# Linear attention followed by a phase-mixing block on one core: two more batches' x, and one more batch's u, turned by DMA instead of TensorE, part of the absolute values on ScalarE, and a new instruction order

## The chip, the core and the metric

The kernel runs on one core of a Trainium2 chip. The metric is the device time of one execution in microseconds (us), here the median of a few executions. The core has five engines with queues of their own, each of which works strictly in order: TensorE (PE, with its weight loads as PEld), VectorE (DVE), ScalarE (ACT), GpSimd (POOL) and SyncE (SP). SP computes nothing; it issues DMA transfers. POOL computes a little and issues the transfers that change the data type. An engine that waits for another holds up everything behind it in its own queue, and the order in those queues is what most of this change alters.

## The reference

All of it is done for 8 batches with 8 heads, 576 rows and 64 columns per head; the channel width C is 512.

```python
kv  = einsum('bhsd,bhse->bhde', k, v)          # 64x64 per head
o   = einsum('bhsd,bhde->bhse', q, kv)
x   = o / sqrt(mean(o*o) + 1e-6) * g_norm      # per head; then heads side by side: 576 x 512
th  = x @ w_theta
zr, zi = x * cos(th), x * sin(th)
y   = w_tok_r @ zr + w_tok_i @ zi              # mixes the 576 rows
u   = x + y
out = u + maximum(u @ w_ch, 0)
```

## The kernel before, in words

A batch's 576 rows are cut into four tiles of 128 rows (numbered 0 to 3) and a tail of 64 rows (tile 4, kept with its two halves of columns on 128 partitions). Each batch goes through these steps; the word in brackets is the name used below, followed by the tile that the profile shows and the line.

- The transfers of k and v (tiles kt and vt, lines 200 and 206 for the full rows and the tail rows) go out on SP into two buffers each, so batch b can be loaded once the key-value product of batch b-2 is done. q comes by POOL (qh and qe, lines 212 and 218), which turns it into fp16, into three buffers.
- The key-value product (kv, line 285, 80 small matmuls per batch) and its copy out of PSUM (kbd, lines 307 and 309).
- q is turned: by TensorE in batches 0 and 1, by a DMA transpose on SP from batch 2 on (qD, line 330).
- The raw product (raw, lines 344 and 353) into one of only two PSUM buffers; its square on ACT (sqb, 366), the row sums on DVE (ss, 375), the inverse root on POOL (rt, 382), and the scaling on DVE that gives x (405 and 414) and frees the PSUM buffer.
- x is turned so that its channels lie on partitions. Batches 0 to 4 do it with four TensorE transposes per full tile and two for the tail (xps, line 302). Batches 5 to 7 do it with DMA transposes on SP (xd, line 433): one for tiles 0 and 1, one for tiles 2 and 3, one for the tail. A copy that multiplies by g follows (xT, lines 257 and 259).
- The phase product (th, lines 464 and 467); then on ACT the rounding to whole turns (pt, 480), on DVE the remainder (arg, 486) and its absolute value (arg, 494), on ACT sine (sc, 502) and cosine (sc, 509), on DVE the product with x (zm, 531). The tail's parts are moved by small POOL transfers (zt, 537).
- The token mix (y, line 554): eight output pieces per batch, each made of nine matmuls that are issued in three parts of three. The first part needs the z of tiles 0 and 1, the second that of tile 2, the third tile 3 and the tail. DVE adds x and gives u (wn, 569).
- The channel product (v, lines 464 and 467). Its sum with u needs u turned back: by four TensorE transposes (ups, line 302) and a copy on ACT (us, 588), or, for the full tiles of batches 5 and 6, by a DMA transpose on SP (ud, line 596) while ACT takes max(v, 0) out of PSUM (vs, 601). DVE adds the two (617 and 612) and SP stores the result (625 and 629).

One list of numbers, TURNS (lines 29 to 81), sets the order. Each number is a task of the list above for one batch and tile; `play` calls the tasks in that order, and so each engine's queue gets its share in that order. A letter behind a number (A, D, P) moves a task that may run on several engines to ACT, DVE or POOL; `r14` means 14 matmuls without use, which keep TensorE's clock up. A task that is called early waits in its queue until its inputs and its buffer are there, and holds up what stands behind it.

`XD` (line 144) is the first batch whose x is turned by DMA, `UD` (line 145) the batches whose u is. xd and qD take their buffers from the same ring of four.

Of the kernel before, what the change touches and what calls it, by code (L numbers as in the profile page):

```python
# [12 lines left out]
AFT = mybir.ActivationFunctionType  # L13
# [17 lines left out]
36 55 50 42 51 37 52 38A 12 56D 53 54 21 63 71 57 64D 43 72 58 73 65 74 44 r2 137 133 59 45 75 46 60  # L31
66 76 138A 134A 61 62 67 77 68 79 89 125 90D 69 70 126 80 r5 91 107 92 108 81D 78 93 98 82 116 117D
94 99 83 95 118 100 129 127 84 85 119 96 86 101 128 87 130 102 120 97 121 88 109 139 141 171 159 122
110 104 123 140 142A 103 124 111 112 105 28 29 26 22 206 27 207 208 30 201 163 135 131 202 113 136
114 106 132D 115 203 204 155 r2 172 160 161 229 173 164 165 156 215 216 162 174 230 166 167 157 147
148 143 168 169 144 158 170 222 145 185 209 210 211 212 149 151 213 186 223D 214 146 150 152 217 231
236 153 243 218 232 237 244 219 154 220 233 205 388 366 377 187 190 175 234 357 188 221 177 192 224
191 176 178 235 225 250 226 251D 238 259 358 227 239 260D 240 193 353 354 514 355 194 356 189 195
252 180 261 196 253 181 262 228 254 245 360 361 241 255 242 263 264 268 362 363 246 256 257 265 266
364 365 247 269D 258 248 359 249 270 286 277 389 271 390 287D 278 288 182 267 391 272 273 183 279  # L40
315 367 289 274 392 275 290 393 291 276 378 311 280 292 293 281 282 379 283 323 312 319 320 430 316
324 284 368 431 294 501 525 502 536 503 504 179 285 369 317 313 318 314 380 505 370 381 321 307 308
325 303 322 326 371 304 305 309 299 300 432 310 382 403 394 433 306 404D 395D 342 301 372 383 396
373 384 397 302 374 434 435 405 347 197 508 509 510 511 406 348 436 437 385 398 407 399 408 438 198
375 386 441 440 439 506 442 295 296 344 400 343 401 513 512 409 376 387 345 402 412 515 526 297 421
422D 298 413 516 410 414 337 423 332 339 349 517 411 415 338 527 416 417 350 528 418 424 419 507 518
529 653 519 425 426 340 530 656 657 658 659 451 542 520 427 428 660 521 420 661D 522 334 537 459 452
662 523 429 543 538 333 335 524 460 453 471 472 473 551 454 539 540 531 461 455 532 552 474 673 684
346 649 650 184 651 652 533 541 456 467 457 468 469 663 534 462 458 535 470 578 327 553 664 328 554
665 579D 463 674 464 560 666 654 465 580 675 555 561D 466 676 556 557 581 558 667 582 677 562 544  # L50
563 583 564 565 685 447 448 329 490 569 545 584 686 566 567 570 585 491 443 449 444 445 546 559 678
687 450 586 446 330 688 571 690 492 668 689 547 691 572 548 669 341 821 810 336 475 679 477 726 573
568 574 727D 670 493 655 589 590 587 588 801 671 797 331 798 832 799 800 494 804 476 575 680 478 681
699 805 806 807 497 728 495 700 549 809 550 808D 496 576 729 682 701 485 692 498 672 730 577 731 480
599 600 591 811 592 593 702 481 486 683 703 822 717 607 601 812 693 705 704 694 594 602 813 814 732
733 823 696 608 603 609 604 605 595 718D 610 734 815 606 824 719 596 597 708 619 735 825 738 802 720
709 706 598 721 695 707 620 615 616 710 621 611 833 826 711 834 697 612 613 623 617 622 722 835 618
836 736 803 737 837 712 698 713 614 625 628 487 816 827 482 714 624 828 817 715 488 626 829 818 483
716 950 629 723 724 838 479 956 872 943 951 952 953 643 767 819 725 847 644 955 820 954D 763 751 764
752 768 769 765 747 748 830 749 638 957 753 831 766 770 873D 754 750 958 839 959 962 848 630 755 960  # L60
484 967 855 489 627 978 944 849 963 756 757 874 850 851 964 631 840 945 946 875 852 639 841 758 961
876 965 947 739 743 740 744 741 968 745 759 842 877 966 742 856 969 853 878 746 970 864D 879 760 640
# [3 lines left out]
895 907 897 898 899 985 904 908 983 896 993D 977 986 889 890 1096 987 900 988 1097 994 891 885 1098  # L66
892 909 1107 1099 995 1108 1018 1001 632 989 996 1109 1110 786 886 913 887 914 888 1100 997 990 1019
998 991 999 1002 1010D 782 915 910 911 1101 1020 783 916 912 1111 992 352 775 1117 637 199 1003 1118
793 937 1102 1021 1022 1023 784 1011 1004 1024 1103 1005 794 499 780 642 1123 917 796 785 648 1104
1025 1012 1119 918 928 923 1026 1013 1120 1006 1014 1105 1007 787 919 1008 924 929 1000 1132D 788  # L70
# [4 lines left out]
1160 1034 1141D 1139 1150 1142 940 1161 1162 935 1151 1152 1074 1163 1143 1164 1084 1144 1085 1069  # L75
# [27 lines left out]
def kernel(  # L103
# [12 lines left out]
    nc = tc.nc  # L116
# [24 lines left out]
    NX, NXE = 7, 4  # L141
    QD = 2

    XD = 5
    UD = (5, 6)

    ZD = 2
    NKV = 2
# [340 lines left out]
        )  # L489
        arg_sb[b, j] = arg  # L490

    def even_arg(b, j):
        arg = arg_sb[b, j]
        nc.vector.tensor_scalar(  # L494
            out=arg[:, 1, :].bitcast(I32), in0=arg[:, 0, :].bitcast(I32),
            scalar1=0x7FFFFFFF, scalar2=None, op0=ALU.bitwise_and,
# [401 lines left out]
```

## Time and profile before

| | |
|---|---|
| median of 3 executions | 221.31 us (220.44 to 221.79) |
| the profiled execution | 221.22 us, of which 219.4 us span from its first to its last instruction |
| TensorE | 204.7 us busy (93%) |
| VectorE | 175.5 us busy (80%) |
| ScalarE | 132.2 us busy (60%) |
| GpSimd | 97.4 us busy (44%) |
| moved by DMA | 43.43 MB, 198 GB/s on average |

The profile names work by line and by tile, `out<-in`. A row of the chain of waits gives a start, a duration, the engine, the tile, the line and the number of instructions. A row of the table of stretches gives for each engine the busy time with the number of instructions, then the clock that TensorE was granted and the busy share of the 16 DMA engines. That share adds up transfers that overlap on an engine, so it can pass 1. A row of SP's own instructions gives the time that SP took to issue a transfer, not the time of the transfer; the list of transfers gives the median from issue to landing.

### The profile page before, as it was taken

Reading aid. Unit: us, or ns where it says so; the run is one execution under the profiler, and the core shown is the slowest. Engines: PE = TensorE matmul, PEld = TensorE weight load, DVE = VectorE, ACT = ScalarE, POOL = GpSimd, SP = SyncE. Lnnn points to the kernel's source line nnn. Section 1 sums busy time; section 2 is a strip of 40 time slices with the busy share of each in tenths; the row PEclk is TensorE's granted clock in tenths of the full one; section 3 lists DMA queues with packets and bytes.
Section 4 is the critical chain, followed back from the end, with each engine's and each line's share of the span. In section 5 each row is a group of like instructions: output and inputs, shape, how many; then the busy total and the mean of one; then the engine's idle time right before and its main releaser. Section 6 shows DMA issues by size and latency. Waiting matters only on the chain.

```text
span 219.4 us, 5548 instructions
## 1 busy us (share of the span) xinstructions
PE 204.7 (93%) x2198; PEld 138.7 (63%) x2198; DVE 175.5 (80%) x371; ACT 132.2 (60%) x268; POOL 97.4 (44%) x102
## 2 busy tenths in 40 slices
PE   7996999899799999989999999999999999999991
PEld 2574456685466667756668866867587746756850
DVE  4029559518989989898999988999997999999662
ACT  2036589306599159663788845848765888557050
POOL 8227830004933529555749067534824544204000
PEclk9998599999999999999999999999999999999999
DMA  6999999965979999979999947996990776944474
GB/s 222 270 291 239 236 229 234 281 163 96 261 109 230 283 176 259 144 81 332 292 224 251 200 131 147 244 241 174 210 138 15 204 207 163 182 110 120 113 262 154
DMA packets 70059, 43.43 MB, mean 198 GB/s; under 512 B 39570, under 2 KB 63762, under 8 KB 70034
## 3 DMA queue, kind: packets, MB, share of 16 engines
q1 hardware_dynamic: 55602, 35.73, 65.5%
q0 software_dynamic: 14432, 7.36, 24.5%
q8 instruction: 17, 0.28, 0.5%
q14 instruction: 8, 0.07, 0.1%
HBM read 33.06 MB, written 9.44 MB: 194 GB/s over the span
## 4 chain that ended last, share of the span: by engine, by line
PE 61%; DVE 13%; DMA 8%; POOL 7%; ACT 7%; issue 2%; POOLq 0%; DVEq 0%; ACTq 0%
PE y L554 26%; PE v L464 10%; PE th L464 9%; DMA wn<-in_moe_w_tok_i_dram 8%; POOL rt L382 5%; PE kv L285 5%; DVE arg L486 2%; DVE ss L375 2%; PE ups L302 2%; PE raw L344 2%; DVE x L405 2%; DVE zm L531 2%; ACT sc L502 1%; PE v L467 1%; POOL qh L212 1%
## 5 line engine op out<-in xcount | busy, mean ns | idle before, releaser
L382 POOL TENSOR_TENSOR rt<-ss,mhalf 128x8 f32<-128x8 f32 (+1 forms) x35 | 54.9, 1573 | 80.5 <-DVE ss L375 78.8
L554 PE MATMUL y<-wT,zm 128*128 128x256 f16 (+1 forms) x512 | 76.0, 286 | 1.5 <-DVE zm L531 1.0
L554 PEld LDWEIGHTS <-zm 128*128 128x128 f16 x512 | 47.7, 98 | 16.9 <-DVE zm L531 2.5
L569 DVE SCALAR_TENSOR_TENSOR wn<-y,gcol,xT 128x256 f16<-128x256 f32 (+2 forms) x72 | 32.5, 477 | 8.2 <-PE y L554 7.6
L480 ACT ACTIVATE pt<-th 128x512 f32<-128x512 f32 (+1 forms) x40 | 21.9, 553 | 21.2 <-PE th L464 13.2
L464 PE MATMUL th<-wth,xT 128*128 128x512 f16 x128 | 32.9, 384 | 0.3 <-DVE xT L259 0.2
L464 PE MATMUL v<-wch,wn 128*128 128x512 f16 x128 | 31.6, 379 | 0.0
L486 DVE SCALAR_TENSOR_TENSOR arg<-pt,th 128x512 f32<-128x512 f32 (+1 forms) x40 | 24.9, 627 | 4.4 <-ACT pt L480 4.1
L509 ACT ACTIVATE sc<-arg,quarter 128x512 f16<-128x512 f32 (+1 forms) x40 | 27.1, 677 | 1.2 <-DVE arg L494 1.1
L502 ACT ACTIVATE sc<-arg 128x512 f16<-128x512 f32 (+1 forms) x40 | 23.4, 588 | 6.9 <-DVE arg L486 6.6
L366 ACT ACTIVATE sqb<-raw 128x512 f32<-128x512 f32 x32 | 18.6, 593 | 14.5 <-PE raw L344 13.2
L405 DVE TENSOR_TENSOR x<-raw,rt 128x512 f16<-128x512 f32 x32 | 21.8, 684 | 3.0 <-POOL rt L382 2.6
L375 DVE TENSOR_REDUCE ss<-sqb 128x8 f32<-128x520 f32 x32 | 21.8, 685 | 2.5 <-ACT sqb L366 2.3
L531 DVE TENSOR_TENSOR zm<-x,sc 128x1024 f16<-128x1024 f16 x32 | 21.8, 682 | 0.5 <-ACT sc L509 0.5
L617 DVE SCALAR_TENSOR_TENSOR us<-v,us 128x512 f32<-128x512 f32 (+1 forms) x32 | 19.4, 616 | 2.0 <-PE v L467 0.8
L307 ACT CAST kbd<-kv 64x256 f16<-64x256 f32 (+1 forms) x28 | 9.4, 335 | 18.5 <-PE kv L278 11.8
L588 ACT ACTIVATE us<-ups 128x512 f32<-128x512 f16 (+1 forms) x32 | 17.0, 541 | 4.1 <-PE ups L302 2.6
L537 POOL DMA_DIRECT2D zt<-zf x24 | 13.7, 576 | 12.2 <-PE v L467 10.9
L464 PEld LDWEIGHTS <-xT 128*128 128x128 f16 x128 | 11.5, 99 | 11.7 <-issue 1.3
L464 PEld LDWEIGHTS <-wn 128*128 128x128 f16 x128 | 11.8, 98 | 11.2 <-issue 0.6
L285 PE MATMUL kv<-vt,kt 128*64 128x64 f32 x560 | 18.3, 223 | 0.0
L554 PE MATMUL y<-wT,zt 128*128 128x320 f16 (+1 forms) x64 | 18.3, 286 | 0.0
(78 smaller groups left out, 256.5 us busy)
## 6 DMA issues: line engine op xcount, KB each, us to landing
kt<-in_k_dram SPq DMA_DIRECT2D x7, 1024.0 KB, 10.4
vt<-in_v_dram SPq DMA_DIRECT2D x7, 1024.0 KB, 8.5
out_dram<-us SPq DMA_DIRECT2D x24, 256.0 KB, 3.2
qh<-in_q_dram POOLq DMA_DIRECT2D x7, 512.0 KB, 7.7
out_dram<-vs SPq DMA_DIRECT2D x8, 256.0 KB, 2.3
zm<-in_moe_w_ch_dram SPq DMA_DIRECT2D x1, 1024.0 KB, 11.0
out_dram<-us SPq DMA_DIRECT2D x16, 64.0 KB, 2.1
kt<-in_k_dram SPq DMA_DIRECT2D x7, 128.0 KB, 6.9
```

What stands on the lines that cost most here:

```text
L285: nc.tensor.matmul(t[i * D:(i + 1) * D, hp - lo, :], kt[b % NKV][:, 2 * hp + i, j, :], vt[b % NKV][:, 2 * hp + i, j, :], start=(j == 0), s ...
L375: nc.vector.reduce_sum(out=ss[:], in_=sq_sb.pop((b, j))[:], axis=AXX)
L382: nc.gpsimd.tensor_tensor(out=rt[:], in0=ss[:], in1=mhalf[:, 0:h], op=ALU.pow)
L405: nc.vector.tensor_tensor(out=x_pair[b, p][:, :, a * HC:(a + 1) * HC].rearrange("p t (h e) -> p h t e", e=D), in0=r[:].rearrange("p (h t e ...
L464: nc.tensor.matmul(t[:], lhs(kc), w[:, kc, :], start=first, stop=last)
L480: nc.scalar.activation(out=pt[:], in_=th_ps[b, j][:], func=AFT.Copy, bias=MAGIC)
L486: nc.vector.scalar_tensor_tensor(out=arg[:, 0, :], in0=pt_sb.pop((b, j))[:], scalar=MAGIC, in1=th_ps.pop((b, j))[:], op0=ALU.subtract, op1 ...
L502: nc.scalar.activation(out=sc[:, 0, :], in_=arg_sb[b, j][:, 0, :], func=AFT.Sin, bias=0.0, scale=-TURN * SHRINK,)
L509: nc.scalar.activation(out=sc_sb[b, j][:, 1, :], in_=arg_sb.pop((b, j))[:, 1, :], func=AFT.Sin, bias=quarter[:], scale=-TURN * SHRINK,)
L531: nc.vector.tensor_tensor(out=dst, in0=x.unsqueeze(1).broadcast_to((P, 2, w)), in1=sc[:], op=ALU.mult)
L554: nc.tensor.matmul(t[:, 0:hi - lo], s, wT[:, w, lo:hi], start=n == 0, stop=n == len(z) - 1)
L569: nc.vector.scalar_tensor_tensor(out=dst, in0=y_in, scalar=gcol[:, 0:1], in1=x_in, op0=ALU.mult, op1=ALU.add,)
```

## The change

The computation stays as it is. Four things change.

1. `XD` goes from 5 to 3: x of batches 3 and 4 is turned by SP's DMA transposes too. That takes 8 full tiles and 2 tails away from TensorE (36 transposes) and adds four large and two small transposes to SP.
2. `UD` gets batch 4: its four full tiles of u are turned by DMA (16 TensorE transposes fewer, four DMA transposes more), and ACT takes max(v, 0) out of PSUM in place of copying u.
3. The absolute value may run on ACT. TURNS puts 15 of the 32 full tiles and 7 of the 8 tails there.
4. TURNS is new from batch 0's raw products on. Other choices move with it: 9 pairs of kbd copies on DVE where there were 4, 6 of the 9 copies of the turned token weights on DVE where there were 3, one of the four w_ch conversions on ACT (it was on POOL), and 30 matmuls without use in place of 38, all of them ahead of batch 0's weight transposes.

```diff
-    XD = 5
-    UD = (5, 6)
+    XD = 3
+    UD = (4, 5, 6,)
...
-    def even_arg(b, j):
+    def even_arg(eng, b, j):
         arg = arg_sb[b, j]
+        if eng == "ACT":
+            nc.scalar.activation(out=arg[:, 1, :], in_=arg[:, 0, :], func=AFT.Abs)
+            return
         nc.vector.tensor_scalar(
...
-            ab = add(f"ab{w} {b} {j}", "DVE", lambda b=b, j=j: even_arg(b, j), [ar])
+            ab = add(f"ab{w} {b} {j}", "DVE", lambda e, b=b, j=j: even_arg(e, b, j), [ar],
+                     alt=("ACT", "DVE"))
...
-0 1 8 4 5 6 7 2 18 3 9 10 11 14 15 r14 31 r15 39 32 47 13 16 17 24 25 33 40 34A 48 23 19 20 35 49 41
+0 1 8 4 5 9 6 7 10 2 11 14 15 13 18 r12 31 16 3 23 19 20 17 r13 39 32 40 47 33 35 48 34A 12 49 41 24
...
```

What the new order does to single queues is seen in two places. (The lines behind 494 are three or four higher after the change.) The first is POOL behind batch 0, where it computes the inverse roots rt of batch 1; qh and qe are loads of q, wch the conversions of w_ch, the MEMSETs clear the unused rows of k and v. Before:

```order
L218 DMA qe_73<-in_q_dram 64x4x64 x2
L259 TENSOR_SCALAR wch<-zm_77 128x512
L248 MEMSET kt_64 64x8x64
L248 MEMSET vt_66 64x8x64
L382 TENSOR_TENSOR rt<-ss,mhalf 128x8 x2
L212 DMA qh_68<-in_q_dram 128x8x256
L218 DMA qe_71<-in_q_dram 64x4x64
L382 TENSOR_TENSOR rt<-ss,mhalf 128x8 x2
```

After:

```order
L218 DMA qe_73<-in_q_dram 64x4x64
L259 TENSOR_SCALAR wch<-zm_77 128x512 x2
L218 DMA qe_71<-in_q_dram 64x4x64
L259 TENSOR_SCALAR wch<-zm_77 128x512
L382 TENSOR_TENSOR rt<-ss,mhalf 128x8 x4
L212 DMA qh_68<-in_q_dram 128x8x256
```

The two q loads that stood between the second and the third root of batch 1 now stand ahead of the first and behind the fourth.

The second place is SP where it loads batch 5 (kt_65 and vt_67, the full rows 128x8x256 and the tail rows 64x8x64). Before, the transposes of batch 4's q (qh_69, qe_72) stood ahead, and nothing but a store (out_dram) between the loads:

```order
L330 DMA_TRANSPOSE qD<-qh_69 128x8x128 x2
L330 DMA_TRANSPOSE qD<-qe_72 128x2x128
L625 DMA out_dram<-us 128x512
L200 DMA kt_65<-in_k_dram 128x8x256
L206 DMA kt_65<-in_k_dram 64x8x64
L625 DMA out_dram<-us 128x512
L200 DMA vt_67<-in_v_dram 128x8x256
```

After, all of batch 3's x transposes (xd) are among them, the first of them ahead of batch 4's q, and the next load (vt_66, batch 6) stands behind batch 4's first two:

```order
L433 DMA_TRANSPOSE xd<-x 128x8x128
L206 DMA kt_65<-in_k_dram 64x8x64
L330 DMA_TRANSPOSE qD<-qh_69 128x8x128 x2
L330 DMA_TRANSPOSE qD<-qe_72 128x2x128
L206 DMA vt_67<-in_v_dram 64x8x64
L433 DMA_TRANSPOSE xd<-x 128x8x128
L433 DMA_TRANSPOSE xd<-x 128x2x128
L628 DMA out_dram<-us 128x512
L200 DMA kt_65<-in_k_dram 128x8x256
L200 DMA vt_67<-in_v_dram 128x8x256
L433 DMA_TRANSPOSE xd<-x 128x8x128
L433 DMA_TRANSPOSE xd<-x 128x2x128
```

So batch 5's k and v are asked for only when x of batch 3 is complete. The other loads stand likewise: k of batch 6 behind the transpose of batch 4's x tiles 2 and 3, k and v of batch 7 behind that of batch 5's; and ahead of batch 3's k and v now stands v of batch 4, which waits for batch 2's key-value product. On PE, batch 1's key-value product comes behind 12 of batch 0's 24 token-mix parts, where it came behind 20.

More of the change, by code (lines that the diff above doesn't have):

```diff
@@ L29 @@
 TURNS = """
-0 1 8 4 5 6 7 2 18 3 9 10 11 14 15 r14 31 r15 39 32 47 13 16 17 24 25 33 40 34A 48 23 19 20 35 49 41
[L31 to L59, printed above, removed]
@@ new lines @@
+50 36 42 51 55 43 25 52 63 56 37D 64 38 71 26 53 72 54 65 44 201 73 66 45 46 57 58 67 74 59 68 75 60
+206 69 61 70 r5 137 207 62 125 138A 126 76 89 79 80 90D 81D 98 77 133 99D 21 78 107 134A 108 116 22
+359 91 117D 30A 82 92 93 129 83 100 94 95 84 96 208 118 130 203 86 27 85 127 97 101 141 128D 28 87
+102 109 119 358 88 103A 131 142 29 104 171 132D 105 135 120 110 159 106 139 121A 136D 122 163 111
+140 160 123 112 229 172 113 124 164 114 204 155 230D 156 115 215 236 173 237 165 216 174 157 161 209
@@ new lines @@
+274 391 275 290 311 392 183 323 291A 368 282 315 276 319 283 369 284 324 316 393 292 370 285 312 293
+353 378 294 430 320 379 355 431 514 380 313 325 314 381 321 326 317 371 299 300 318 383 295 382 189
+384 307 525 296 385 308 394 322 372 386 297 395D 194 373 301 309 302 403 342 374 396 343 501 298 375
+502 310 432 397 404D 508 433 398 347 509 652 434 400 376 510 399A 387 511 401 349 348 513D 436 197
+435A 303 512D 437 304 305 350 515 438 526 198 516 412 439 337 402 405 338 440 517 413 441 339 306
@@ new lines @@
+406 505 332 527 407 421 414 333 518 340 422 344 408 415 528 409 423 651 519 410 416 334 529 424 418
+425 327 520 654 335 521 506 426A 655 530 442 417A 656 411 507 419 657 345 653 427 531 522 346 455
+532 459 420 542 523 428 471 658D 456 659 460 648 429 472 328 463 533 660 473 524 464 534 457 474 671
+461 458 537 543D 465 462 538 682 551 544 539 535 540 552 650 545 466 559 546 661 467 662 541 468 553
+469 663 576 547A 672 554 451 664 673 452 329 184 674 548 647 470 453 556 555A 675 447 330 649 443
@@ new lines @@
+577 444 454 549 445 568D 448 665 449 550 495 683 578 450 684 496 569 446 579 560D 557 676 490 570
+475 685 561 688 491 580 686 558 581A 485 562 666 477 667 687 571 582 722 492 583 563 476 677 584 795
+497 573 478 586 336 565 800 498 587 341 564A 493 801 588 566 806 802 668 585 572A 803 697D 723D 669
+574 567 794 724 805 804D 698 331 828 725 678 597 726 598 699 575 613 817 480 700 614 615 679 702 593
+616 689 680 594 599 701A 690 600 728 670 703 595 727A 609 691 596 589 681 590 729 617 692 705 618
@@ new lines @@
+898 977 906 775 1102 978 907 770 885 899 979 777 1092 902 908 903 886 351 981 989D 887 900 990 1006
+1014 904 1093 982 991 1094 640 893 888 782 983 1095 894 992 1103 881 780 1104 882 771 883 1015 984
+781 998 895 909 1105 994 1113 1016 1096 986 1106 910 993A 896 635 911 884 995 999 776 912 1017 352
+985 783 1000 918 1018 1107 987 1007 996 784 1119 914 1001 1008 1020 1002 933 1019 1114 1009 789 1021
+1097 915 919 790 1022 1115 1026 1003 1116 924 1120D 1004 1117 1128D 988 1129 920 785 1023 925 929
```

29 lines of the change are left out of this document (20 added, 9 removed), and 17 rows, old and new, of the table TURNS.

## The prediction

> **What bounds the kernel now.** I read the page's totals and its slices first, then busy time by stretches, then the chain of waits, then SP's queue and the transfers.
>
> ```profile
> PE 204.7 (93%) x2198; PEld 138.7 (63%) x2198; DVE 175.5 (80%) x371; ACT 132.2 (60%) x268; POOL 97.4 (44%) x102
> DVE  4029559518989989898999988999997999999662
> PEclk9998599999999999999999999999999999999999
> DMA  6999999965979999979999947996990776944474
> ```
>
> TensorE is busiest, DVE close behind, the DMA slices are full for the first three quarters, and the clock drops once. A busy TensorE isn't one that works without gaps, since matmuls overlap. So I price its work and compare it with the time. These rows of the chain give the prices (its last three, and the first for the key-value product), the places of three key-value products, and one wait:
>
> ```profile
> 46.34 2.51 PE kv L285 x80
> 50.58 0.36 PE raw L344 x3
> ...
> 55.73 0.93 POOL qh L212
> 56.66 0.65 POOL qe L218
> 57.31 3.50 POOL rt L382 x2
> 60.83 0.69 DVE x L405
> ...
> 115.92 0.73 PE kv L285 x20
> ...
> 137.42 2.52 PE kv L285 x80
> ...
> 178.51 4.32 PE v L464 x20
> ...
> 199.98 8.82 PE y L554 x72
> ...
> 209.67 0.45 PE ups L302 x8
> ```
>
> A transpose costs 0.45/8 = 0.056, a token-mix part (three matmuls) 8.82/72 x 3 = 0.37, a full theta or channel product (four) 4.32/20 x 4 = 0.86 (a tail taken as half of it), a batch's key-value product 2.5; a raw product, four matmuls of a transpose's shape, 0.225. The stretches below begin at batch 0's token mix (35.3) and then at the key-value products of batches 1, 2, 3, 4, 5, 6, 7, up to the last matmul; the first two rows are the slow clock and what follows it.
>
> ```profile
> 20.60:27.50 6.90, 6.24 (x31) 3.32 (x32) 4.39 (x11) 3.23 (x7) 5.95 (x7) 0.51 1.13 238
> 27.50:34.30 6.80, 6.36 (x54) 3.73 (x52) 4.45 (x9) 6.20 (x13) 1.72 (x3) 1.00 1.28 239
> 35.30:46.30 11.00, 10.29 (x90) 7.65 (x90) 7.28 (x16) 4.91 (x9) 0.00 (x0) 1.00 1.24 268
> 46.30:59.90 13.60, 11.76 (x165) 8.13 (x166) 9.43 (x18) 6.93 (x15) 7.46 (x6) 1.00 0.65 150
> 59.90:81.60 21.70, 20.34 (x248) 14.10 (x248) 19.86 (x43) 13.86 (x29) 8.66 (x8) 1.00 1.04 197
> 81.60:90.80 9.20, 9.05 (x143) 6.61 (x141) 8.21 (x17) 9.01 (x21) 7.72 (x9) 1.00 1.17 226
> 90.80:115.90 25.10, 23.62 (x274) 16.48 (x268) 23.33 (x47) 16.26 (x33) 14.45 (x13) 1.00 1.06 225
> 115.90:137.40 21.50, 21.50 (x255) 15.70 (x254) 20.02 (x43) 14.26 (x29) 12.94 (x14) 1.00 0.89 178
> 137.40:159.70 22.30, 22.30 (x245) 15.52 (x246) 21.21 (x42) 15.72 (x32) 12.59 (x12) 1.00 0.95 215
> 159.70:214.10 54.40, 54.40 (x498) 36.58 (x496) 47.82 (x103) 33.79 (x67) 15.62 (x16) 1.00 0.64 152
> ```
>
> TensorE's work by these prices, in program order, is 9.3, 11.1, 18.6, 8.9, 22.5, 21.2, 22.2 and 54.0 us, where the stretches last 11.0, 13.6, 21.7, 9.2, 25.1, 21.5, 22.3 and 54.4. So TensorE waits 7.3 us in the first three, 2.9 in the next two, and 0.8 in the 98 us from batch 5 on, where it is the bound. The early waits are those for the chain raw, square, sums, root, x: in the chain two q loads of 0.93 and 0.65 stand between POOL's roots, and the x behind them comes at 60.83. Those waits, not TensorE's work, are the largest thing that an order can win.
>
> **The change part by part.** The sum is made against the profiled execution, 221.22 us, with a span of 219.4 and 1.8 around it; the median is 221.31, the same within 0.1.
>
> *Transposes off TensorE.* 36 of x and 16 of u, 52 x 0.056 = 2.9 us, nearly all of it behind 46 us. From batch 5 on nothing else covers this work, and before that it stands in a queue that is 94% busy: -2.9 (ends 0 and -2.9). The same work by stretches becomes 6.2, 13.4, 17.9, 11.7, 20.7, 17.2, 23.3 and 54.4. The matmuls without use that go stood in waits (for loads and for ACT) and cost nothing; what they did for the clock is a rival below.
>
> *Start.*
>
> ```profile
> L307 ACT COPY wT<-wps 128x576 f16<-128x576 f16 x6 | 3.7, 641 | 1.1 <-PE wps L643 1.0
> ```
>
> In batch 0's sine stage, where ACT is busy 6.20 of 6.80 us, it loses three copies of turned weights (0.641 each) and one of x, which DVE takes in its idle time; that is some 2 us of ACT's queue ahead of batch 0's last cosine and z. I take -1.3, ends 0 and -2.
>
> *Batch 1 sooner.* Its key-value product comes behind 12 token-mix parts instead of 20, 8 x 0.37 = 2.9 us sooner, and these eight parts now lie in the second stretch, where TensorE waited 2.5 us. The q loads leave the gap between the roots (0.93 + 0.65). So the waits of the first two stretches (1.7 + 2.5) nearly close; the 3.1 of the third stay, because DVE is 92% busy there. I take -4.1; ends 0 (DVE sets the pace anyway) and -7.3 (all waits go).
>
> *Absolute values and copies.*
>
> ```profile
> L494 DVE TENSOR_SCALAR arg<-arg 128x512 int32<-128x512 int32 (+1 forms) x40 | 15.7, 396 | 0.6
> L480 ACT ACTIVATE pt<-th 128x512 f32<-128x512 f32 (+1 forms) x40 | 21.9, 553 | 21.2 <-PE th L464 13.2 <-PE th L467 7.8
> L309 DVE CAST kbd<-kv 64x256 f16<-64x256 f32 x8 | 3.4, 421 | 3.6 <-ACT kbd L307 3.4
> ```
>
> 22 absolute values leave DVE, 22 x 0.396 = -8.7; five pairs of kbd copies come, 10 x 0.421 = +4.2, and three weight copies of about 0.45. DVE gains some 3 us net. An absolute value on ACT isn't in the trace; the nearest row is ACT's own copy of the same shape, 0.553, so ACT gets 22 x 0.553 = 12.2 and gives back about 5. ACT was 66% busy from 116 to 137 and stays under 75%. From batch 5 on TensorE covers both engines; I take 0. If that cover is gone, the cosine comes 0.16 later per absolute value, at most 3.5; if DVE is what holds batches 1 to 4, up to 3 come back. u of batch 4 trades an ACT copy for an ACT maximum of the same size: 0.
>
> *New transfers and new waits.* SP issues ten transposes more.
>
> ```profile
> 67.59 0.56 SPq L200 DMA_DIRECT2D kt<-in_k_dram  x1
> 68.27 6.66 SPq L330 DMA_TRANSPOSE qD<-qh  x1
> ...
> 132.71 1.28 SPq L433 DMA_TRANSPOSE xd<-x  x1
> ```
>
> ```profile
> DMA to landing us min/median/max: 5.9/8.5/21.2
> ```
>
> ```profile
> kt<-in_k_dram SPq DMA_DIRECT2D x7, 1024.0 KB, 10.4
> vt<-in_v_dram SPq DMA_DIRECT2D x7, 1024.0 KB, 8.5
> qD<-qh SPq DMA_TRANSPOSE x12, 5.7
> xd<-x SPq DMA_TRANSPOSE x9, 3.3
> ```
>
> The first rows are SP's queue, the next the view of line 200 (loads of k and v), the last the list of transfers. Undisturbed, a transpose costs SP 1.28 us and lands 3.3 us after its issue; right behind a 1 MB load SP took 6.66. Loads need 5.9 to 10.4 us, their median 8.5. For each wait I set the new chain against the TensorE work that stands between its start and the product that needs it:
>
> - k and v of batch 3 now go behind v of batch 4, a tail and a store, all of which wait for batch 2's key-value product: issued about 5 us behind it, landed at 13.5 to 15.4, needed after 15.4 of work (21 parts 7.7, five full products 4.3, two tails 0.9, small ones 2.5) and some 2 of waits. 0 to 1.5; I take 0.5.
> - Theta of batch 3 needs xd. From the channel product that DVE's x stands behind: four DVE steps of 0.68, a store of 0.5, landing 3.3, copy 0.7, so 7.2 against 7.8 of work. 0 to 2; 0.5. Behind it on SP, q of batch 4: 8.3 to 10.8 against 9.6, 0 to 1.5; 1.0. On DVE the copy of xd for tile 3 holds up batch 4's first x: 0 to 2.5; 0.5.
> - k and v of batch 5 wait in SP for xd of batch 3's tail: from that tail's raw product 6.0 to the issue (DVE takes it behind theta of tile 0: part and theta 1.2, pt 0.55, arg 0.63, x and queue 0.9; SP's transpose 1.3, store 0.5, two loads 1.0), 14.5 to 16.4 to the landing, against 13.7 of work (13 parts 4.8, seven full products 6.0, two tails 0.9, small ones 2.0). 0.8 to 2.7, less the waits above, which delay the product as well: 0.5.
> - k of batch 6 stands behind the transpose of batch 4's tiles 2 and 3: from the raw product 11.9 to the issue (8.3 of TensorE's work up to a token-mix piece that DVE adds first, 0.5, x 0.7, transpose 1.3, a tail's load and k 1.1), 17.8 to 22.3 to the landing (5.9 to 10.4), against 17.7 (24 parts 8.8, the key-value product 2.5, five full products 4.3, two tails 0.9, small ones 1.1). 0.1 to 4.6; 1.5. Batch 7 likewise (8.3 to the issue): 16.8 to 18.7 against 18.2; 0 to 0.5; 0.5.
>
> Together +5.0, ends 0 and about 15. Stores and the moves of zt behind these transfers fill buffers that have several us to spare.
>
> Sum: -2.9 - 1.3 - 4.1 + 5.0 = -3.3, so a span of 216.1 and a time of 217.9 us, 1.5% less.
>
> **The rivals.**
>
> *SP's queue becomes the bound (slower).* The place is 85 to 150 us, where a batch's loads, q, x and stores share SP and DMA. For it: there the DMA share is already 0.9 to 1.2; one transpose behind a load took SP 6.66 us; now xd of batch 4 stands directly behind two loads of 1 MB, and batch 6's v behind it. Against it: the share falls between bursts (0.65 and 0.89 in two stretches), and the new work is about 12 us of issuing (ten transposes at 1.2) over 100 us. The price: if four of the new transposes on the path take 3 us more than 1.28 to issue, the waits are 17 instead of 5, and the time is 229 or, where they partly overlap, about 226. It decides once the waits pass 8.3 us. The Trainium skill (VectorE: DVE Perf Modes, "Rules for kernel authors" and "The three transpose paths") speaks for this side: a 128x128 transpose belongs on TensorE where PSUM will do as the destination, at 390 ns against 1309 ns by DMA. By its figures the 52 blocks would be 68 us of transfers, an estimate; here eight blocks land in 3.3 us, so the trace doesn't agree with the size, and TensorE's 0.056 is far below its figure too.
>
> *The clock stays low longer.* At 20.6 to 27.5 the clock was 0.51 while TensorE transposed and waited; five matmuls without use stood there ahead of theta, and they are gone. If the low clock lasts another 6.9 us, some 4 us of theta, weight transposes and first token mix take twice as long, of which ACT, busy 6.20 of those 6.80 us, covers a part: 0 to +4, I take +3, so 220.9. Against it: batch 0's matmuls ahead of the low stretch are denser now. By the Trainium skill (TensorE: Matmul & The Clock Gate, "Part 4: PE-mode transpose") transposes don't count as busy for the clock; this trace agrees as far as its one low stretch holds mostly transposes.
>
> *DVE holds the early batches,* so that bringing batch 1 forward wins only 1 of the 4.1: 221.0. For it: 19.86 busy of 21.7 in the third stretch. Against it: DVE idled 3.7 of 11.0 in the first and 4.2 of 13.6 in the second.
>
> *Everything is hidden:* the waits are 0.5 instead of 5: 213.4.
>
> **How the numbers follow.** My forecast has 0.46, SP's queue 0.25, the clock 0.07, DVE 0.10, everything hidden 0.12. The forecast's own range is 215 to 220.5. Under 1% is about what a measurement of this kernel can't tell from no change; faster by more than that means under 219.1, slower means over 223.5. Faster: 0.40 of the forecast and all of the hidden case, 0.52. Within 1%: 0.06 of the forecast, 0.09 of DVE, 0.05 of the clock, 0.04 of SP's queue, 0.24. Slower: the rest, 0.24. The range leaves out the strongest form of SP's queue and the outer end of the hidden case: 213.0 to 225.0.
>
> **What would show it.** Right: batch 1's key-value product starts 4 us or more ahead of 46.3 and batch 3's 5 us or more ahead of 81.6; xps and ups rows are 52 matmuls fewer; no stretch from batch 5 on has TensorE idle over 2 us; DVE's arg row of absolute values falls to 18. Wrong: TensorE's waits in front of a key-value product are put down to a kt or vt transfer, or in front of theta to xd, with more than 8.3 us together; SP's transposes take 3 us or more to issue between 85 and 150; or a second stretch of clock 0.5 behind 27.

## The result, and the profile after the change

The changed kernel takes 222.29 us (median of 20 runs, 220.34 to 225.62), the kernel before 220.94 us beside it (median of 20, 218.89 to 222.2). The ratio is 1.0057 with a 95% interval of 1.0029 to 1.0085: 0.6% slower, within what I had called no difference, and not the 1.5% less of the forecast. A ratio here is always to the kernel before on the same chip and leaves disturbed runs out, so it can differ from the quotient of two medians.

The profiled execution of the changed kernel, 220.34 us with a span of 218.5, is the fastest of its 20 runs, so the trace shows 2 us less than the median. The page's totals, and TensorE's granted clock in 40 slices:

```profile
PE 197.7 (90%) x2138; PEld 133.2 (61%) x2138; DVE 172.8 (79%) x366; ACT 139.5 (64%) x278; POOL 95.2 (44%) x101
...
PEclk9999799999999999999999999999999999999997
```

TensorE is busy 7 us less and the span is 0.9 us shorter: nearly all that was taken off TensorE came back as waits. The stretches, cut as in the prediction (batch 0's token mix, then each key-value product), with the columns span, PE, PEld, DVE, ACT, POOL, clock, DMA share, GB/s:

```profile
33.30:40.20 6.90, 6.56 (x59) 4.85 (x58) 5.51 (x13) 5.11 (x11) 1.49 (x1) 1.00 1.35 218
40.20:54.00 13.80, 13.47 (x193) 10.35 (x194) 10.58 (x21) 6.89 (x13) 5.81 (x4) 1.00 0.92 207
54.00:73.70 19.70, 19.03 (x237) 13.05 (x231) 19.02 (x41) 13.83 (x31) 9.93 (x8) 1.00 1.02 247
73.70:85.20 11.50, 11.50 (x169) 8.26 (x165) 10.84 (x22) 10.31 (x21) 7.46 (x9) 1.00 1.02 195
85.20:111.00 25.80, 22.19 (x250) 14.88 (x248) 22.19 (x45) 18.53 (x39) 13.32 (x14) 1.00 1.13 199
111.00:129.70 18.70, 17.53 (x204) 12.67 (x204) 15.35 (x31) 15.39 (x31) 10.88 (x13) 1.00 1.09 244
129.70:155.60 25.90, 23.88 (x254) 16.35 (x254) 22.55 (x47) 16.82 (x34) 12.71 (x11) 1.00 1.08 219
155.60:213.30 57.70, 55.20 (x488) 36.06 (x490) 47.66 (x103) 35.76 (x69) 17.33 (x19) 1.00 0.76 158
```

Batch 3's key-value product starts at 73.7 where it started at 81.6, so it comes 7.9 us sooner in these two executions; some 1.5 us of that is the clock and not the order (see *Start* below). The five stretches behind it last 11.5, 25.8, 18.7, 25.9 and 57.7 us, for work that the prediction had put at 11.7, 20.7, 17.2, 23.3 and 54.4. So TensorE waits 5.1, 1.5, 2.6 and 3.3 us in the last four, where it had waited 3.7 us in all behind batch 3's product (times and work as in the prediction), and of the lead 0.9 us are left at the end. The waits that TensorE got are named by the view of waits (engine, tile, line, releaser; us in total, times, longest):

```profile
PE kv L285 <- DMA vt<-in_v_dram: 3.1, 2, 1.6
PEld kv L285 <- issue: 3.0, 3, 1.8
PE th L464 <- DVE xT L259: 2.1, 2, 1.7
PE kv L285 <- DMA kt<-in_k_dram: 0.9, 1, 0.9
```

Before, no key-value product waited for a transfer. Their chain runs through SP and the DMA engines; in the chain of waits the long pieces of the late half are transfers:

```profile
88.42 5.23 DMA xd<-x
...
110.87 6.18 DMA zt<-zf
...
122.83 6.77 DMA kt<-in_k_dram
...
145.63 9.82 DMA vt<-in_v_dram
...
175.78 3.92 DMA xd<-x
```

And SP's queue shows why k and v were asked for so late. Batch 5's stand behind the two transposes of x at 96.31, batch 6's k behind the one at 120.84:

```profile
96.31 3.76 SPq L433 DMA_TRANSPOSE xd<-x  x2
...
100.75 0.42 SPq L200 DMA_DIRECT2D kt<-in_k_dram  x1
101.21 0.68 SPq L200 DMA_DIRECT2D vt<-in_v_dram  x1
...
120.84 1.23 SPq L433 DMA_TRANSPOSE xd<-x  x1
...
122.83 0.60 SPq L200 DMA_DIRECT2D kt<-in_k_dram  x1
```

### The profile page after: what moved, and what is told of

The parts are those of the page before. It is cut to its first block, busy times and chain, and to the rows that moved or that the text cites. A ratio compares the mean times of both kernels' runs of the same rounds, so it can differ in the third digit from the quotient of the medians.

```text
span 218.5 us, 5445 instructions
## 1 busy us (share of the span) xinstructions
PE 197.7 (90%) x2138; PEld 133.2 (61%) x2138; DVE 172.8 (79%) x366; ACT 139.5 (64%) x278; POOL 95.2 (44%) x101
## 3 DMA queue, kind: packets, MB, share of 16 engines
q1 hardware_dynamic: 62578, 37.43, 72.6%
## 4 chain that ended last, share of the span: by engine, by line
PE 26%; DMA 25%; DVE 24%; POOL 8%; issue 7%; ACT 7%; SPq 1%; POOLq 0%; DVEq 0%; ACTq 0%
PE y L557 11%; DMA wnt<-in_moe_w_tok_i_dram 7%; DMA xd<-x 6%; PE kv L285 5%; DMA vt<-in_v_dram 4%; POOL rt L382 4%; PE th L464 4%; DVE x L405 4%; DMA kt<-in_k_dram 3%; DVE wn L572 3%; DVE arg L486 3%; DVE zm L534 3%; DMA zt<-zf 3%; PE v L464 3%; DVE ss L375 2%
## 5 line engine op out<-in xcount | busy, mean ns | idle before, releaser
L366 ACT ACTIVATE sqb<-raw 128x512 f32<-128x512 f32 x32 | 18.8, 594 | 10.5 <-PE raw L344 10.4
L591 ACT ACTIVATE us<-ups 128x512 f32<-128x512 f16 (+1 forms) x28 | 14.9, 536 | 14.0 <-PE ups L302 11.8
L540 POOL DMA_DIRECT2D zt<-zf x24 | 13.1, 551 | 21.7 <-PE th L464 6.4
L285 PEld LDWEIGHTS kv<-vt,kt 128*64 128x64 f32 x560 | 17.4, 138 | 4.8 <-issue 3.0
L557 PE MATMUL y<-wT,zt 128*128 128x256 f16 (+1 forms) x64 | 18.3, 286 | 0.4 <-DMA zt<-zf 0.2
L307 ACT CAST kbd<-kv 64x256 f16<-64x256 f32 (+1 forms) x18 | 6.2, 342 | 18.1 <-PE kv L278 10.6
```

Of the source, the lines that this page charges most:

```text
L285: nc.tensor.matmul(t[i * D:(i + 1) * D, hp - lo, :], kt[b % NKV][:, 2 * hp + i, j, :], vt[b % NKV][:, 2 * hp + i, j, :], start=(j == 0), s ...
L557: nc.tensor.matmul(t[:, 0:hi - lo], s, wT[:, w, lo:hi], start=n == 0, stop=n == len(z) - 1)
```

## The experiments

The kernels are numbered in the order in which they ran.

**Is the early gain real, and where is it given back?** Theory W: the gain up to batch 3 is real, and new late waits take it. Rival D: from batch 3 on other resources set the pace, so an early lead melts under any order. e1 follows the changed order up to batch 3's last key-value piece (task 511) and takes every later task in the old order, without the new transfers:

```diff
-    XD = 3
-    UD = (4, 5, 6,)
+    XD = 5
+    UD = (5, 6)
...
-376 510 399A 387 511 401 349 348 513D 436 197 435A
+376 510 399A 387 511 505 303 304 305 306 435 405
```

> The changed order up to batch 3's last kv, and from there the old order with x turned by transfers from batch 5 on and u in batches 5 and 6. Theory W (the early gain is real, and is given back by new waits from batch 4 on, for k and v and for x turned by transfers): the changed kernel starts batch 3's kv 7.9 us sooner with 1.5 us less of TensorE's work done by then, so about 6.4 us should come through: 214.5 us, 213 to 218. Rival D (from batch 3 on the DMA engines, ScalarE or VectorE set the pace whatever the order, so that an early lead always melts): 220 to 222 us.

Measured: 217.99 us, ratio 0.9891 (0.9848 to 0.9933). By the ratio 2.4 us come through, of the 6.4 that W expected (214.5 us). One reason is a seam: both copies of batch 3's kv stand behind sines and cosines on ScalarE there.

```profile
PE raw L344 <- ACT kbd L307: 2.2, 4, 1.7
```

e8 moves those two copies (tasks 513 and 512) up:

```diff
-505 303
+505 513 512 303
...
-401 513 512 409
+401 409
```

> The first experiment's kernel with the two copies of batch 3's kv moved up on ScalarE, ahead of four pieces of sines and cosines of batch 2, where its raw products waited 1.8 us. If the wait is only that seam of the two orders: 216.5 us, 215.5 to 217.5. If x or the q transposes of batch 3 end as late: 218 us.

Measured: 215.35 us, ratio 0.9759 (0.972 to 0.9797). This beats both kernels, the one before by 5.3 us, and shows that the seam alone cost 2.9. Its late stretches (columns as above):

```profile
85.10:110.10 25.00, 23.55 (x274) 16.44 (x268) 23.30 (x47) 16.20 (x33) 14.61 (x13) 1.00 1.12 221
110.10:131.60 21.50, 21.50 (x254) 15.71 (x252) 20.02 (x43) 14.25 (x29) 13.01 (x14) 1.00 0.87 192
131.60:154.00 22.40, 22.40 (x247) 15.59 (x248) 21.30 (x42) 15.82 (x32) 12.65 (x12) 1.00 0.96 214
154.00:208.30 54.30, 54.30 (x496) 36.47 (x492) 47.68 (x103) 33.61 (x67) 15.53 (x16) 1.00 0.66 152
```

From 110 on TensorE has no gap, as in the kernel before. D falls: under the old late order the lead stays.

e2 is the reverse, the old order up to batch 2's last key-value piece (task 363), then the changed one with its transfers:

```diff
-    XD = 5
-    UD = (5, 6)
+    XD = 3
+    UD = (4, 5, 6,)
...
-264 268 362 363 246 256 257 265
+264 268 362 363 359 536 246 256
```

> The old order up to batch 2's last kv, and from there the changed order with all of its transfers. Theory W: the lead of 6.0 us at batch 2's kv is missing and the late waits stay: 222.3 + 6.0 - 0.8 (work already done by then) = 227.5 us, 225 to 229. Rival D: the late part has its own pace, so about 222 us, 220.5 to 223.5.

Measured: 227.21 us, ratio 1.0221 (1.0148 to 1.0295). The late waits are there without any lead to run into them. By the ratio the loss is 4.9 us, less than W's 6.6 but no zero as for D.

**Can k and v simply be asked for sooner?** The loads of batches 5, 6 and 7 (tasks 647 to 650, 793 to 796, 939 to 942) go up by a stage on SP in e3 and are cut from their old places:

```diff
-522 346
+522 647 648 649 650 346
...
-329 184
+329 793 794 795 796 184
...
-833 834
+833 939 940 941 942 834
```

> The changed kernel with the k and v loads of batches 5, 6 and 7 issued a stage sooner on SP: batch 5's ahead of the store of batch 1 that SP waits on at 76 to 88 us, batch 6's ahead of batch 0's store behind x's transposes of batch 3, batch 7's ahead of x's first transpose of batch 5. Theory W, and that these loads are the main part of the waits: the stalls ahead of kv 5, 6 and 7 (1.7, 1.1 and 1.7 us) close, 218 us, 217 to 220. Rival C (the DMA engines' capacity, not SP's order: the loads only collide with other transfers): 222 to 224 us.

Measured: 231.53 us, ratio 1.0496 (1.0465 to 1.0526). My own mending made it 9 us worse; C had the direction, and both were too kind. Two of its stretches, then a row of its chain:

```profile
93.00:101.00 8.00, 0.90 (x6) 0.38 (x4) 0.69 (x1) 0.17 (x1) 1.64 (x1) 0.63 1.44 178
101.00:107.00 6.00, 6.00 (x34) 3.13 (x33) 3.80 (x8) 1.61 (x4) 1.01 (x1) 0.64 0.62 112
```

```profile
88.48 12.01 DMA zt<-zf
```

TensorE stands still for some 7 us for a move of zt, 32 KB, which POOL issues and not SP. It lands 12.01 us after its issue, because k and v of batch 5 are on the same DMA engines (share 1.44). The same move landed after 4.8 us in the changed kernel, there too right behind the same loads of q on POOL. So this wait doesn't arise in SP's queue. The Trainium skill (DMA: Bandwidth & Descriptors, "Issuing engines are not separate DMA queues") says that transfers of all issuers run on the same 16 engines and interleave; this trace agrees. Behind the stall the clock is 0.64 for another 6 us of full work, which costs about 2 us more (an estimate: 6 x 0.36).

One could say that a whole stage is too much. So e16 moves only the three loads that stand right behind a transpose: k of batch 6 (793), k and v of batch 7 (939, 941).

```diff
-795 497
+795 793 497
...
-952 636
+952 939 941 636
```

> The changed kernel with three loads moved up on SP: k of batch 6 from behind x's transpose of batch 4's tiles 2 and 3 (122.8 us) to behind v of batch 6 (109.5), k and v of batch 7 from behind x's transpose of batch 5's tiles 2 and 3 (145) to behind q's first transpose of batch 6 (137). If SP's order makes the waits: those ahead of kv 6 and kv 7 (1.1 and 1.7 us) close and nothing comes instead, 219.5 us, 218.5 to 220.5. If the DMA engines' load makes them: q of batch 5, the moves of zt of batch 3 and x of batch 5 land as much later, 222.3 us, 221 to 225.

Measured: 225.99 us, ratio 1.0214 (1.0153 to 1.0275). The waits ahead of kv 6 and kv 7 did close. The first fence is the view of waits, where 1.2 us in one piece are left (batch 5's), the second the chain. The traced execution, 228.47 us, is the longest of the six, so its sizes are rather too large:

```profile
PE kv L285 <- DMA vt<-in_v_dram: 1.2, 1, 1.2
```

```profile
113.78 7.04 DMA zt<-zf
...
143.35 8.76 DMA out_dram<-us
```

But a store of 256 KB behind batch 7's two loads now needs 8.76 us; ScalarE's copy of u waits for its buffer, VectorE's sum for that, and TensorE 4.1 us for the sum. In both kernels sooner loads delayed what stands behind them and lost more than they won: in these stretches the DMA engines have no time to spare. (In e16 the store stands behind the loads on SP as well, so that queue could also be the cause; e3's move of zt stands on POOL.)

**What are stores worth?** To take load off the DMA engines without touching SP's queue, the full tiles' stores of batches 0 to 3 write one row of 128:

```diff
+        rows = 1 if b < 4 else P
...
-                out=out[b, 0:SM, :].rearrange("(p j) c -> p j c", j=NJ)[:, j, :], in_=ot[:]
+                out=out[b, 0:SM, :].rearrange("(p j) c -> p j c", j=NJ)[0:rows, j, :],
+                in_=ot[0:rows, :],
```

e6, in the changed kernel:

> The changed kernel, whose stores of batches 0 to 3 write one of 128 rows only (the tails' stores stay whole), so that the issues stay on SP and some 4 MB of the 45 MB go: part of the result is not written. Theory C (the DMA engines' time is short between 75 and 160 us): loads and transposes land sooner and the late waits shrink, at least 3 us under the changed kernel, 217 to 219 us. Rival L (SP's order and the flight of each transfer set the waits): within 1 us of 222 us.

e7, in the kernel before:

> The kernel before with the same thin stores of batches 0 to 3, as a measure of what they are worth there: part of the result is not written. Theory C: the kernel before has DMA time to spare, so 0 to 1 us off, 219.5 to 220.5 us. If stores cost SP or the end of the kernel the same in both, it falls by as much as the changed kernel does.

Measured: 219.80 us, ratio 0.9956 (0.9923 to 0.999), and 220.29 us, ratio 0.9962 (0.9933 to 0.9991). The changed kernel gains 2.2 us (1.0057 to 0.9956), less than C's 3 and more than L's 1, so neither had the size; the one before gains 0.8. So fewer bytes help the changed kernel more, by 1.4 us, uncertain by about 1.2. The changed kernel's waits with thin stores show why it isn't more:

```profile
PEld L557 <- DMA zt<-zf: 2.4, 2, 2.1
...
PE kv L285 <- DMA kt<-in_k_dram: 1.3, 1, 1.3
PE kv L285 <- DMA vt<-in_v_dram: 0.3, 1, 0.3
```

The wait for v shrinks from 3.1 to 0.3, and the moves of zt of batch 3, hidden until then, become the next wait.

**Which transfers?** e4 has batch 3's x alone back on TensorE:

```diff
-    XD = 3
+    XD = 4
```

> The changed kernel with batch 3's x turned on TensorE again (18 transposes, close ahead of their copies), all else as changed. Theory W: 18 x 0.056 = 1.0 us of TensorE more, against some 0.5 to 2 us of waits for theta of batch 3: 222 us, 221 to 223. Rival X (the flight of x through the transfers, 5.2 us from issue to landing for batch 3, is what the lead is lost to): batch 3's theta starts some 3 us sooner and that is kept, 219 us, 218 to 220.

Measured: 221.87 us, ratio 1.0024 (0.9985 to 1.0064), which can't be told from the changed kernel. Again zt takes the place of the waits that went:

```profile
PE y L558 <- DMA zt<-zf: 3.4, 2, 2.1
```

e14 has x of batches 3 and 4 there, with u of batch 4 still by transfers (and two copies of batch 2's u moved up on ScalarE, so that the buffers suffice):

```diff
-    XD = 3
+    XD = 5
```

> The changed kernel with x of batches 3 and 4 turned on TensorE and u of batch 4 still by transfers; two copies of batch 2's u moved up on ScalarE. TensorE gets 36 x 0.056 = 2.0 us more. If x's transfers are the main cost, through theta and through the k and v loads of batches 5 and 6 behind them: 219 us, 218 to 221. If u's are: 222.3 + 2.0 = 224 us, 222.5 to 225.

Measured: 217.96 us, ratio 0.9865 (0.9814 to 0.9916): 1.9% or 4.2 us under the changed kernel, though TensorE has 2.0 us more to do. It also moves two copies on ScalarE, whose own worth wasn't measured. SP's queue, and all of PE's and PEld's waits of key-value products from batch 1 on:

```profile
96.52 0.42 SPq L201 DMA_DIRECT2D kt<-in_k_dram  x1
96.99 4.49 SPq L201 DMA_DIRECT2D vt<-in_v_dram  x2
...
114.50 0.63 SPq L201 DMA_DIRECT2D kt<-in_k_dram  x1
```

```profile
PEld kv L286 <- DVE arg L487: 0.3, 1, 0.3
PEld kv L286 <- issue: 0.3, 1, 0.3
```

Batch 5's k goes out at 96.5 instead of 100.8, batch 6's at 114.5 instead of 122.8, and no key-value product waits for a transfer. The loads don't land faster, they are asked for sooner. The lists of transfers (median to landing), first the changed kernel, then this one:

```profile
kt<-in_k_dram SPq DMA_DIRECT2D x7, 1024.0 KB, 7.3
vt<-in_v_dram SPq DMA_DIRECT2D x7, 1024.0 KB, 9.7
```

```profile
kt<-in_k_dram SPq DMA_DIRECT2D x7, 1024.0 KB, 7.8
vt<-in_v_dram SPq DMA_DIRECT2D x7, 1024.0 KB, 10.7
```

So here it was the place of x's transposes in SP's queue, ahead of the loads, that delayed k and v. What x costs the DMA engines is in the page's list of queues (packets, MB, share of 16 engines' span), first the changed kernel, then this one:

```profile
q1 hardware_dynamic: 62578, 37.43, 72.6%
```

```profile
q1 hardware_dynamic: 57778, 36.25, 66.9%
```

72.6% of 218.5 are 158.6 us, 66.9% of 216.4 are 144.8: with x of two batches, 1.18 MB, the queue's packets take 13.8 us more of all 16 engines. But this share adds up packets that overlap on an engine, so it grows with crowding as well. The two other pairs of kernels that differ by these transfers show 3.1 us (e9 to e13, 67.1% of 218.5 to 67.6% of 221.5) and 7.4 (e12 to e5, 68.3% of 215.7 to 63.3% of 244.4), and e9 and e15, with the same transfers, differ by 5.2 (64.2% of 220.2). So x takes between 3 and 14 us there, and these runs don't settle it better.

e9 has u of batch 4 on TensorE too (with four of its sums on VectorE moved up, for the same reason):

```diff
-    XD = 3
-    UD = (4, 5, 6,)
+    XD = 5
+    UD = (5, 6)
```

> The changed order with the change's transfers undone: x of batches 3 and 4 and u of batch 4 turned on TensorE, put close ahead of their copies, two copies of batch 2's u and four final products of batch 4 on VectorE moved up so that the buffers in PSUM suffice; abs stays partly on ScalarE. TensorE gets 52 x 0.056 = 2.9 us more. Theory T (the transfers' flights and what they take from the loads make the late waits): the waits ahead of kv 5 to 7 and of theta fall by more than 2.9 us, 219 us, 217 to 221. Rival O (the late order itself waits): 222 + 2.9 = 225 us, 223 to 226.

Measured: 219.78 us, ratio 0.993 (0.9899 to 0.996), as T expected. But O has a share too: e8 has the same matmuls and no more transfers, and is 3.8 us faster (uncertain by 1.1). What differs is the late order, and more abs on ScalarE; but without these e9 gets slower still (e15 below). From 85 us on TensorE waits 5.0 us in e9 by the view of waits, all of it for VectorE and ScalarE, and 1.4 us in e8. The longest in e9:

```profile
PE y L558 <- DVE us L621: 1.3, 1, 1.3
PE v L465 <- DVE us L621: 0.7, 1, 0.7
PE th L465 <- ACT xT L258: 0.7, 2, 0.5
```

e13 has u of batch 4 alone on TensorE, and x by transfers (of that diff the lines of UD only):

> The changed kernel with u of batch 4 alone turned on TensorE (its four final products on VectorE moved up so that the buffers in PSUM suffice), x of batches 3 and 4 still by transfers. TensorE gets 16 x 0.056 = 0.9 us more. If u's transfers, with the copy of the final product that ScalarE then makes behind TensorE, are the main cost: 219.5 us, 218.5 to 220.5. If x's transfers are: 222.3 + 0.9 = 223 us, 222 to 224.

Measured: 223.83 us, ratio 0.9994 (0.9939 to 1.0049), with runs from 220.15 to 226.6. e13 is inconclusive: its ratio rests on three of its twelve runs, and its median is 1.1% above that of the kernel before. By the ratios e14, with u's transfers, is 1.4 us faster than e9, uncertain by 1.3. So in the new order u's transfers are no clear loss and at best a small gain. They are a loss in the old late order, where e12 adds them to e8:

```diff
-    UD = (5, 6)
+    UD = (4, 5, 6)
```

> The eighth experiment's kernel with u of batch 4 alone turned by transfers, issued where TensorE turned it. Theory T, whose loss comes from x's transfers in front of theta and of the loads: u stands late enough (four tasks to over a hundred before the final sum that needs it), so 16 x 0.056 = 0.9 us come off or are lost to small waits, 214.4 to 215.6 us. If any transfer added between 150 and 175 us brings waits of its own: 216 to 219 us.

Measured: 218.89 us, ratio 0.9889 (0.9839 to 0.9939), by the ratios 2.9 us more than e8. ScalarE's waits for a channel product, in e8 and then in e12:

```profile
ACT vs L604 <- PE v L464: 7.9, 1, 7.9
```

```profile
ACT vs L604 <- PE v L464: 10.9, 3, 8.0
```

With u turned by DMA, ScalarE copies the channel product instead of the turned u, and must wait for it. Two such waits, 3 us, now stand in ScalarE's queue. That they make the whole difference was only read from the trace.

e5 puts all of the change's transfers into e1, close to where TensorE's transposes stood:

```diff
-    XD = 5
-    UD = (5, 6)
+    XD = 3
+    UD = (4, 5, 6,)
```

> The first experiment's kernel (changed order up to batch 3's kv, old order behind it) with the change's transfers put into the old late order: x of batches 3 and 4 and u of batch 4 turned by transfers, each issued as soon as its rows are made, the copies of x and of u moved behind them. Theory T (the transfers themselves bring the late waits, by their flight and by what they take from the loads): no better than the first experiment's 218.0 us, 219 to 223. Rival O (it is the new late order; the transfers alone give what they take off TensorE): 218.0 - 52 x 0.056 = 215.1 us, 214 to 217.

Measured: 244.69 us, ratio 1.1073 (1.1025 to 1.112). Neither theory had that size; T had the direction. Two of its stretches:

```profile
105.00:116.00 11.00, 0.30 (x3) 0.18 (x4) 0.52 (x2) 0.41 (x1) 1.40 (x1) 0.67 1.07 261
116.00:122.00 6.00, 6.00 (x41) 3.02 (x40) 5.85 (x13) 4.29 (x9) 1.68 (x1) 0.75 0.01 3
```

The tail's transpose of batch 3 stood behind batch 5's loads, was issued at 109.1 and landed at 115.4, and theta waited 11 us. That says how far transfers must be re-timed; what a good order would lose, this kernel doesn't tell.

**Abs on ScalarE.** e10 is the changed kernel without its 22 A's on abs:

```diff
-88 103A 131
+88 103 131
...
-139 121A 136D
+139 121 136D
```

> The changed kernel with every abs on VectorE as before, the order unchanged. If the abs on ScalarE costs nothing, as the prediction had it: 222 us, 221 to 223. If ScalarE's extra 7 us (139.5 busy against 132.2) delay the copies of x that theta waits for: 1 to 3 us sooner, 219 to 221. If VectorE is short of time in the late part: 223 to 226 us.

Measured: 223.80 us, ratio 1.0096 (1.0058 to 1.0133), no gain from taking them off ScalarE (0.9 us more, uncertain by 1.0). e15 does the same to e9:

> The ninth experiment's kernel (transfers of the change undone, 219.8 us) with every abs on VectorE as well: only the changed order is left, from batch 0 to the end. If the new late order is what is left to lose against the old one behind the same early part (215.35 us): within 1 us of 219.8 us, 219 to 221. If abs on ScalarE is: 217 us, 216 to 218.

Measured: 221.68 us, ratio 1.0018 (0.9987 to 1.0049), 0.9% more than e9 and above both ranges. e11 adds to e8 the 18 A's that it lacks:

```diff
-306 435 405
+306 435A 405
...
-416 417 350
+416 417A 350
```

> The eighth experiment's kernel (215.35 us: the changed order up to batch 3's kv, the old one behind it, two copies moved up) with the 18 abs that the changed kernel has on ScalarE from batch 2's rear on, put there without moving anything. If abs on either engine is hidden: 215.4 us, 214.8 to 216. If it delays ScalarE where TensorE waits for it: 216 to 218 us.

Measured: 217.61 us, ratio 0.9844 (0.98 to 0.9888), 0.85% or 1.9 us more than e8. So abs on ScalarE helps in the order made for it (e9 against e15) and hurts in the one that wasn't.

## Why the prediction was wrong, step by step

- *Transposes off TensorE, -2.9.* The count was right (52 matmuls of xps and ups went). But the transfers that take their place have a price: without those of x the kernel is 4.2 us faster, though TensorE has 2.0 us more to do (e14).
- *Start, -1.3.* Batch 0's token mix begins at 33.29 instead of 35.27, 2.0 sooner, but most of that is luck with the clock. From 20.6 to 27.5 it was 0.51 in the traced execution of the kernel before and 0.80 in that of the changed one. In other traces of either order it isn't low there at all, as in e7, which has the old order (clock in 40 slices; the fifth is this stretch):

```profile
PEclk9999999999999999999999999999999999999998
```

At such a clock the old order begins the mix at 33.45 and 33.59 (e7, e2), the new one at 32.60 to 33.48 (e8, e13, e1, e14). So the order wins some 0.5 us, and 1.5 are the clock.
- *Batch 1 sooner, -4.1.* In the first three stretches the waits fall from 7.3 to 2.9 us, by 4.4. The sum is right, its parts less so: the first two stretches give 3.1 where I had taken nearly all of 4.2, and the third, which was to stay, gives 1.3. Both steps together were to bring 5.4 us, and e8, which has them without the late half, brings 5.3; that they agree so well is partly luck, with the start smaller and the third stretch better.
- *Absolute values, 0.* An absolute value takes 0.555 us on ScalarE by the profile's row, against my 0.553; in the changed order they cost nothing that could be measured (1.0096 without them, 1.0057 with).
- *New waits, +5.0.* This is the step that failed. By the prediction's own prices the waits behind batch 3's key-value product grow from 3.7 to 12.3 us in the traces, so by 8.6. Two things were wrong in it.
  - Its places were mostly right, their sizes not. By the view of waits, batch 5's and batch 7's loads cost 1.5 and 1.6 us, where I had taken 0.5 each; batch 6's 0.9 against 1.5; theta of batch 3 0.4 against 0.5; the raw product of batch 4's tail 0.9, for DVE's x, against 1.0 for its q. The loads landed as I had priced them (those that TensorE waited for after 6.8 to 9.8 us, against 5.9 to 10.4). They were asked for late: v of batch 5 went out 8.3 us behind the raw product of batch 3's tail, not 6.0, because two transposes stood ahead of it and held SP for 3.76 us, where I had counted one of 1.3. Batch 7's theta, 1.7 us, and its token mix, 0.4, I hadn't listed at all, since its x was turned by DMA before as well. There the transpose landed at 180.35 and theta began at 183.21; now it lands at 179.70, and TensorE waits for it from 178.7.
  - I had priced waits for the new transfers only and taken the new order's own at nothing ("From batch 5 on TensorE covers both engines"). e9 has that order without the new transfers and is 3.8 us slower than e8, which has the old late order. There TensorE doesn't cover VectorE's sums and ScalarE's copies, but waits 5.0 us for them.
- *The rivals.* SP's queue came nearer than my forecast. Its point of decision, 8.3 us of new waits, is what the 8.6 just pass (those put down to kt, vt and xd alone are 6.1 in the view of waits). Its price wasn't right: SP took 1.2 to 3.6 us to issue a transpose from 85 on, and no four of them were 3 us late by that. And SP's order isn't the whole of it, since loads that go out sooner make other transfers late (e3, e16) and fewer bytes help (e6). How much of x's price is its place in SP's queue and how much the DMA engines' time, no run separates: e14 takes both away. The clock's low stretch didn't last longer, 0.80 instead of 0.51 in the same 6.9 us. DVE didn't hold the early batches.

The experiments split the result as follows, as differences of ratios times 221 us: the early half -5.3 (e8, 0.9759); the new late order with abs and u's transfers +2.3 (e14, 0.9865; without u's transfers it is +3.8, e9); x's transfers +4.2 (1.0057), which is net of the 2.0 us of work that they take off TensorE. By the intervals the second and third are certain to about 1.4 us each. Of the 4.4 us between the forecast and the changed kernel's median the traces show 2.4. The other 2.0 lie between that kernel's profiled run and its median, and aren't explained; its 20 runs spread over 5.3 us, those of the kernel before over 3.3, which would fit waits on transfers but wasn't tried. Whether another late order could hide x's transfers stays open too: two ways of mending it on SP failed.

## What to carry to other kernels

Before moving work from a compute engine to the DMA engines, read the DMA share in the stretch where it lands, and what stands behind it in the queue that issues it. Here the share was 1.1 where x's transposes were added, the loads behind them went out later, and loads that were issued sooner (share 1.44 in e3) delayed the transfers of others. When each of several waits is bounded one by one, add what a closed wait uncovers (here zt behind v) and list the later batches too, even if nothing of theirs was changed but the order. A new order has waits of its own: price it without the new transfers first. And test a change of several parts by splicing old and new orders: the early half alone was worth 2.4%, and the sum had hidden it.

## What the runs showed of the hardware

What DMA transposes take of the DMA engines depends on what runs beside them: 1.18 MB added 3.1, 7.4 and 13.8 us of packet time in three pairs of kernels, where in the changed kernel the whole queue moves 37.43 MB in 158.6 us, 4.2 us per MB. A small transfer of another issuer isn't protected: 32 KB from POOL took 12.01 us next to 1 MB loads (e3), where the median of these moves is 3.8. And a stall costs twice. After TensorE stood still for some 7 us its clock was 0.64 for the next 6 us of work (e3), after 11 us it was 0.75 (e5). The Trainium skill (TensorE: Matmul & The Clock Gate, "What's actually happening") gives about 3.4 us of idling as enough for half rate; the stalls of 7 and 11 us agree, and the waits under 2 us of the changed kernel left the clock at 1.00. Shorter ones aren't always safe: in e13 waits of 1.1 and 2.2 us within 108 to 118.8 were followed by 0.51 from 118.8 to 122.2.
